# Sparse attention and a gated feed-forward layer on one core: early queries and keys in 256-byte pieces on two queues, fewer warming products, probabilities set out by any engine

## The chip, the cores and the metric

The kernel runs on one core of a Trainium2 chip. The time is device microseconds of one execution, and a kernel's time is the median of several. Five engines work side by side: TensorE (PE in the profile; its weight loads are PEld), VectorE (DVE), ScalarE (ACT), GpSimd (POOL) and SyncE (SP, which here only issues transfers). Each runs its own instructions strictly in the order of the program and waits for the others by semaphores.

## The reference

All is float32. The scores reach values at which the softmax is sharp, so the kernel keeps float32 accuracy by splitting each operand of a large product into a high part and a low rest and adding three products (high by high, high by rest, rest by high).

```
q, k, v: (8, 8, 576, 64)            # batch, head, position, width
scores = q @ k.T / 8
heads 0..3: key j counts for query i if 0 <= i - j < 32
heads 4..7: key j counts for query i if j <= i and j % 32 == i % 32
attn = softmax over the keys that count
x = (attn @ v), heads side by side  # (4608, 512)
h = x @ w_in                        # w_in (512, 2048)
g = h * clip(h + 3, 0, 6) / 6
out = g @ w_out                     # w_out (2048, 512)
```

## The kernel before

**Attention** goes by pairs of heads: `pair(g)` makes heads 2c and 2c+1 of batch b, 32 pairs in all. Pairs c = 0, 1 are local (`loc`), c = 2, 3 strided; within a batch they are taken in the order 0, 2, 1, 3 (`TURNS`). Names in the trace carry b and c: `ps_30` is the scores' bank of pair 3, its first head. For a pair, the queries and keys are loaded (`load`), stood upright (for batch 0 by TensorE against an identity, line 371, out of PSUM by the two halves of `evac`; later by DVE), multiplied (`scores`, lines 600 and 608), copied or masked into a tile `e` (lines 626, 633, 640), and made into probabilities in the steps `most`, `less`, `exp`, `total`, `inverse`, `norm` (lines 644 to 665). There are two tiles `e`, one for each head of a pair, and all pairs share them. Then the probabilities are **set out**: turned in 32 x 32 blocks and placed on the diagonal of a cleared tile (`atstr`, `atloc`), so that a few products with the values (line 735 for strided pairs, 399 and 388 for local ones, tile `pv`) give x. Batches 0 and 1 do this by DVE transposes of 32 partitions each, straight into place (`turn`, lines 684 and 687: 4 for a strided head, 6 for a local one). Batches 2 to 7 do it by one transpose in place (`flip`, line 690) and copies on ACT (`spread`, lines 697 and 700). The local pairs of batch 0 (`first`) turn by TensorE (`stand`, tile `pe`). `keep_x` splits x into its high part (ACT, line 426) and its rest (DVE, line 429), in two pieces `n` = 0, 1 for most pairs, and puts the last 64 positions by in `left`.

**Weights** come as raw bits: `weight_part` loads 512 KB (line 273), takes the number apart on ACT (lines 281, 285), joins it on DVE (line 289), casts the high part on ACT or POOL (303, 305) and makes the rest on POOL (308).

**The feed-forward layer** goes by tiles of 512 positions, one tile for each of the batches 0 to 2 (`ffn`), then by larger tiles. `first_product` makes one of 16 slices fc of h, from the four x tiles c (lines 856 to 858, three products of 128 x 512 each); line 776 and 779 are the gate, 790 and 794 the split of g (`gh`, `gl`), 833 to 835 the second product. In batch 0 the first four slices are begun before any is gated.

**The order.** Every step is given to a planner (`Plan`) as an operation with an engine (or a choice of engines), a duration that the author wrote down, the tiles that it reads and writes, and a due time. `emit` then places the operations one by one in its own clock, for each engine the earliest that can start, and the instructions of each engine stand in that order. Where its clock sees PE idle in the first 100 us, it puts in **warming products** (`idle`: once 46 small ones, line 1568, then 128 x 384 ones, line 1570). `T0` is the moment that the plan sets for the first slice of h; all later due times count from it. So a change of costs or keys early on moves instructions on every engine.

**Transfers** take one of eight completion counters in turn, whichever queue they go to. The first eight issue at once; each later one waits in its queue until the transfer eight places before it has landed, and whatever stands behind it on that engine waits too. Transfers of SP and of ACT run on the same 16 DMA engines.

Of the kernel before, what the change touches and what calls it, by code (L numbers as in the profile page):

```python
# [10 lines left out]
F32 = mybir.dt.float32  # L11
# [8 lines left out]
P = 128  # L20
# [17 lines left out]
T0 = 44.0  # L38
# [15 lines left out]
IDLE = 0.64  # L54
FETCH = 2.2
FIRST = 3.4
FEW = 46


class Plan:  # L60
# [29 lines left out]
    def emit(self, idle):  # L90
# [21 lines left out]
        while done < len(ops):  # L112
# [24 lines left out]
            if e == "PE" and t < WARM and t - free[e] > IDLE:  # L137
                for i in range(int((t - free[e]) / IDLE)):
                    order.append((free[e] + i * IDLE, len(order), None, e))
# [34 lines left out]
def attention_ffn(ctx: ExitStack, tc, q, k, v, w_in, w_out, out):  # L174
    nc = tc.nc
# [154 lines left out]
    def either(us):  # L330
        return {"POOL": us, "DVE": us}

    def zero(key, pool, shape, dtype, us, due, name):

        def go(e):
            on(e).memset(new(pool, key, shape, dtype, name), 0.0)
            if key[0] == "e":
                t = tiles[key]
                on(e).memset(t[:, :NQB * WIN].rearrange("p (u x) -> p u x", x=WIN)[:, :, 2 * PAD:], 1.0e-9)
                on(e).memset(t[:, NQB * WIN:NQB * WIN + 8 * PAD].rearrange("p (u x) -> p u x", x=PAD)[:, :, NPOS:NPOS + 1], 1.0e-9)  # L340
        op(either(us), 0, go, writes=[key], due=due)
# [63 lines left out]
    def x_keys(b, c):  # L405
        return [("x", b, c, i) for i in range(2)] if b < 2 else [raw_key(b, c)]

    def keep_x(nm, b, c, puts, due):
# [4 lines left out]
        for n, (bkey, what, place, size, rest) in enumerate(puts):  # L413
# [16 lines left out]
            kk = [lk] if rest else xk  # L430
            last = all(x[0] is not bkey for x in puts[n + 1:])
            whole = rest or b >= 2
            op("ACT", 0.15 + size * (0.0019 if strided else 0.00085), hi, reads=[bkey] + (xk if rest else []), writes=kk, give=bkey if last and whole else None, due=due + n)
            if not whole:
                op("DVE", 0.15 + size * (0.002 if strided else 0.00105), lo, reads=[bkey], writes=kk, give=bkey if last else None, due=due + 0.2 + n)
# [4 lines left out]
    def pair(g):  # L440
# [37 lines left out]
        for x in "qk":  # L478
# [6 lines left out]
            if early:  # L485
# [3 lines left out]
                def load(x=x, nkey=nkey, rows=rows, ni=ni):  # L489
                    t = new(wp, nkey, [P, 2, ni * D], F32, f"{x}n{nm}")  # L490
                    (nc.scalar if g < 2 and x == "k" else nc.sync).dma_start(
                        t[:rows], {"q": q, "k": k}[x][b, h0:h0 + 2].rearrange("j (p i) d -> p j (i d)", i=ni))
                tb = [slot(early) for _ in range(2)]

                def tr(x=x, nkey=nkey, tb=tb, rows=rows, ni=ni):
                    ps = [psum(tb[h], f"{x}p{nm}{h}") for h in range(2)]
                    half = ni // 2
                    for i in range(ni):
                        for j in range(2):
                            upright(ps[i // half], j, i % half * rows, tiles[nkey][:rows, j, D * i:D * i + D])  # L500
# [15 lines left out]
                op("ACT" if g < 2 and x == "k" else "SP", 0.55, load, writes=[nkey], due=-60 + 2 * g + (x == "k") - 900 * (g < 2 and x == "k"), after=1.15)  # L516
# [161 lines left out]
        for j in range(2):  # L678
# [9 lines left out]
            if b >= 2:  # L688
# [16 lines left out]
                op("ACT", 6 * 0.31 if loc else 4 * 0.36, spread, reads=[ekeys[j]], writes=[akeys[j]], due=due - 1.9 + j)  # L705
# [31 lines left out]
        op("PE", 1.25 * slow, values, reads=[*akeys, *vkeys], writes=[*vb, *xk, lk], take=vb, due=due - 1001,  # L737
# [80 lines left out]
    def ffn(b):  # L818
        s0, puts = start[b], []
        chunk = TILE / NFC  # L820
        xk = {c: x_keys(b, c) if b < 2 else [("x", 1, c, i) for i in range(2)] for c in range(NCC)}

# [19 lines left out]
        def first_product(fc):  # L842
# [3 lines left out]
            for n_, c in enumerate(TURNS[b]):  # L846
# [12 lines left out]
                op("PE", 0.683, mm1, reads=xk[c] + wkeys, writes=[pk],  # L859
# [744 lines left out]
```

## Time and profile before

| | us |
|---|---|
| median of 3 runs (869.94, 870.25, 876.99) | 870.25 |
| the profiled execution's own time | 871.98 |
| its span, from the first to the last instruction | 870.2 |
| PE busy | 847.4 |
| POOL, ACT, DVE busy | 616.6, 558.9, 539.0 |
| first transpose of batch 0 on PE | 8.30 |
| first product of h | 38.90 |
| end of the 48 products with which h is begun | 58.88 |

Times in the profile count from the start of the span. A float32 product appears as two passes on PE; its busy time overlaps with the next one's, so PE's speed is read from the distance of starts and not from the durations. A wait in brackets is the idle time of the engine just before the instruction and what ended it; `issue` means that the profile shows nothing that was waited for.

### The profile page before, as it was taken

The page shows a single profiled execution, that of the slowest core. Times are in us where ns is not written, and L with a number is a line of the kernel's source. Part 1 is how long each engine was busy: PE and PEld are TensorE (multiplying, and loading weights), DVE is VectorE, ACT ScalarE, POOL GpSimd, SP SyncE. Part 2 cuts the span into 40 slices and gives each one's busy share as a digit, 9 for nine tenths or more (in the row PEclk, how much of TensorE's full clock was granted, in tenths as well). Part 3 has the DMA queues.
Part 4 walks back from the last instruction along what each step waited for, and adds up shares of the span by engine and source line. Part 5 has one row for each costly group of instructions (what it writes and reads, how often), then busy time and mean ns, then how long its engine had stood idle before and what let it go on. Part 6 is the DMA issues. An engine that isn't in the chain of part 4 may idle for free.

```text
span 870.2 us, 18946 instructions
## 1 busy us (share of the span) xinstructions
PE 847.4 (97%) x6962; PEld 683.8 (79%) x6962; DVE 539.0 (62%) x898; ACT 558.9 (64%) x1246; POOL 616.6 (71%) x606
## 2 busy tenths in 40 slices
PE   8889999999999999999999999999999999999996
PEld 6667777887888788888888878788888778888884
DVE  5688878344454538454546664466767888555586
ACT  3687657678778865877677965776744645454441
POOL 4688877587547799766676994465975987767673
PEclk9999999999999999999999999999999999999998
DMA  8968723898984455898999897877666667866636
GB/s 194 330 138 233 234 41 73 210 281 245 279 234 108 128 129 141 233 266 233 269 277 289 274 301 214 237 204 189 183 202 193 185 180 222 240 202 192 183 122 145
DMA packets 323308, 179.12 MB, mean 206 GB/s; under 512 B 182864, under 2 KB 300368, under 8 KB 323216
## 3 DMA queue, kind: packets, MB, share of 16 engines
q1 hardware_dynamic: 318564, 176.27, 71.5%
q10 hardware_dynamic: 4652, 1.64, 0.9%
q8 instruction: 55, 0.90, 0.4%
q14 instruction: 37, 0.30, 0.1%
HBM read 136.97 MB, written 40.89 MB: 204 GB/s over the span
## 4 chain that ended last, share of the span: by engine, by line
PE 82%; DMA 5%; POOL 5%; DVE 4%; ACT 2%; issue 1%; SPq 0%; POOLq 0%; DVEq 0%; ACTq 0%
PE P L1129 8%; PE P L1130 8%; PE P L1131 8%; PE cP L1452 5%; PE cP L1453 5%; PE cP L1454 5%; PE acc L833 5%; PE ph L856 5%; PE ph L857 4%; PE ph L858 4%; PE acc L835 4%; PE acc L834 4%; PE acc L1214 3%; PE acc L1215 3%; PE acc L1216 3%; PE pv L399 2%
## 5 line engine op out<-in xcount | busy, mean ns | idle before, releaser
L1470 DVE SCALAR_TENSOR_TENSOR C<-cP,C 128x512 f32<-128x512 f32 x96 | 65.7, 687 | 40.4 <-PE cP L1454 39.5
L794 POOL TENSOR_TENSOR gl<-u,gh 128x512 fp32r<-128x512 f32 x48 | 65.2, 1361 | 33.3 <-ACT gh L790 17.1
L1141 DVE TENSOR_TENSOR G<-P,G 128x512 f32<-128x512 f32 x64 | 44.0, 689 | 65.6 <-PE P L1131 53.2
L1129 PE MATMUL P<-B_T,wr 128*128 128x512 f32 x192 | 76.1, 396 | 3.9 <-ACT G L1136 2.3
L833 PE MATMUL acc<-wo,gh 128*128 128x512 f32 x192 | 77.2, 402 | 0.0
L835 PE MATMUL acc<-wo,gl 128*128 128x512 f32 x192 | 75.2, 392 | 0.3 <-POOL gl L794 0.2
L834 PE MATMUL acc<-wo,gh 128*128 128x512 f32 x192 | 74.9, 390 | 0.0
L1130 PE MATMUL P<-B_T,wr 128*128 128x512 f32 x192 | 74.8, 390 | 0.0
L1131 PE MATMUL P<-B_T,wr 128*128 128x512 f32 x192 | 74.8, 390 | 0.0
L1136 ACT COPY G<-P 128x512 f32<-128x512 f32 x64 | 37.6, 587 | 52.2 <-PE P L1131 51.7
L1367 POOL TENSOR_TENSOR sp<-G,sp 128x512 fp32r<-128x512 f32 x34 | 47.6, 1411 | 24.6 <-ACT sp L1363 22.5
L665 POOL TENSOR_TENSOR e<-e,st 128x144 f32<-128x144 f32 (+1 forms) x64 | 44.9, 704 | 20.7 <-DVE st L661 15.2
L779 DVE SCALAR_TENSOR_TENSOR u<-u,ph 128x512 f32<-128x512 f32 x48 | 32.8, 684 | 38.0 <-ACT u L776 37.8
L856 PE MATMUL ph<-x,wi 128*128 128x512 f32 x128 | 52.5, 410 | 2.3 <-ACT x L426 1.2
L857 PE MATMUL ph<-x,wi 128*128 128x512 f32 x128 | 50.8, 397 | 1.4 <-DVE x L429 0.8
L700 ACT COPY atloc<-e 32x192 f32<-32x192 f32 x144 | 50.8, 353 | 1.9 <-DVE e L690 0.3
L776 ACT ACTIVATE u<-ph,three 128x512 f32<-128x512 f32 x48 | 33.0, 687 | 28.1 <-PE ph L858 27.8
L858 PE MATMUL ph<-x,wi 128*128 128x512 f32 x128 | 50.8, 397 | 0.0
L644 DVE TENSOR_REDUCE st<-e 128x8 f32<-128x144 f32 (+1 forms) x64 | 25.6, 412 | 35.8 <-POOL e L640 35.6
L1129 PE MATMUL P<-B_B,wr 128*128 128x512 f32 x120 | 47.1, 392 | 0.0
L1130 PE MATMUL P<-B_B,wr 128*128 128x512 f32 x120 | 46.8, 390 | 0.0
L1129 PEld LDWEIGHTS P<-B_T,wr 128*128 128x128 f32 x192 | 36.0, 188 | 13.7 <-ACT G L1136 3.6
(604 smaller groups left out, 2672.6 us busy)
## 6 DMA issues: line engine op xcount, KB each, us to landing
wr<-dA SPq DMA_DIRECT2D x72, 256.0 KB
or<-do SPq DMA_DIRECT2D x32, 512.0 KB
wr<-dSu SPq DMA_DIRECT2D x48, 256.0 KB
wr<-dSv SPq DMA_DIRECT2D x48, 256.0 KB
or<-do SPq DMA_DIRECT2D x48, 256.0 KB
rawi<-in_moe_w_in_dram SPq DMA_DIRECT2D x16, 512.0 KB
rawo<-in_moe_w_out_dram SPq DMA_DIRECT2D x16, 512.0 KB
do<-wo SPq DMA_DIRECT2D x16, 512.0 KB
```

What stands on the lines that cost most here:

```text
L700: nc.scalar.copy(at[PAD * (a + h):PAD * (a + h) + PAD, :, rows], e[rows, :, PAD * h:PAD * h + PAD])
L794: (nc.vector if tail else nc.gpsimd).tensor_tensor(out=to, in0=src(), in1=tiles[gk[0]].bitcast(F32), op=ALU.subtract)
L833: nc.tensor.matmul(acc, gh, woh, start=fc == 0, stop=False)
L834: nc.tensor.matmul(acc, gh, wol, start=False, stop=False)
L835: nc.tensor.matmul(acc, gl, woh, start=False, stop=end)
L856: nc.tensor.matmul(ph, wih, xh, start=n_ == 0, stop=False)
L857: nc.tensor.matmul(ph, wih, xl, start=False, stop=False)
L858: nc.tensor.matmul(ph, wil, xh, start=False, stop=n_ == NCC - 1)
L1129: nc.tensor.matmul(ph, wh, xh, start=fresh and k == 0, stop=False, skip_group_check=not fresh)
L1130: nc.tensor.matmul(ph, wh, xl, start=False, stop=False, skip_group_check=not fresh)
L1131: nc.tensor.matmul(ph, wl, xh, start=False, stop=k == 1, skip_group_check=not fresh)
L1470: nc.vector.scalar_tensor_tensor(out=tiles[ck], in0=tiles[bank], scalar=1.0 / 6.0, in1=tiles[ck], op0=ALU.mult, op1=ALU.add)
```

## The change

1. The queries and keys of batch 0 are loaded into a tile of [partition, i, head, 64] instead of [partition, head, i x 64], by two transfers of one head each instead of one of both. A contiguous run in the tile is 256 bytes, where it was 1536 (local) or 2048 (strided). The keys of the first three pairs go by ACT's queue, where it was those of the first two.
2. Warming products are counted from 2.6 us on and not from the start of PE's idle time.
3. Strided pairs of batch 0 and all pairs of batch 1 set the probabilities out by `flip` and single copies (4 or 6 a head), each an operation of its own that ACT, POOL or DVE may take, and POOL resets a column of a strided `e` (`again`).
4. The two pieces of an x tile of batches 0 and 1 have keys of their own, so in the plan the second high part does not wait for the first rest, and the copies into `left` are due 3 us later.
5. `T0` is 43 instead of 44.

```diff
-T0 = 44.0
+T0 = 43.0
+FREE = 2
+LEFTS = 3.0
+BEGIN = 2.6
...
-                for i in range(int((t - free[e]) / IDLE)):
+                for i in range(int((t - max(free[e], BEGIN)) / IDLE)):
...
-            kk = [lk] if rest else xk
+            kk = [lk] if rest else xk if whole else [("xh", b, c, n)] + ([] if n else xk)
...
-                op("DVE", 0.15 + size * (0.002 if strided else 0.00105), lo, reads=[bkey], writes=kk, give=bkey if last else None, due=due + 0.2 + n)
+                op("DVE", 0.15 + size * (0.002 if strided else 0.00105), lo, reads=[bkey, ("xh", b, c, n)], writes=[("xl", b, c, n)], give=bkey if last else None, due=due + 0.2 + n)
...
-                    t = new(wp, nkey, [P, 2, ni * D], F32, f"{x}n{nm}")
-                    (nc.scalar if g < 2 and x == "k" else nc.sync).dma_start(
-                        t[:rows], {"q": q, "k": k}[x][b, h0:h0 + 2].rearrange("j (p i) d -> p j (i d)", i=ni))
+                    t = new(wp, nkey, [P, ni, 2, D], F32, f"{x}n{nm}")
+                    for j in range(2):
+                        (nc.scalar if g < 3 and x == "k" else nc.sync).dma_start(
+                            t[:rows, :, j], {"q": q, "k": k}[x][b, h0 + j].rearrange("(p i) d -> p i d", i=ni))
...
-            if b >= 2:
+            if b >= 2 or b == 1 or b == 0 and not loc:
...
-                op("ACT", 6 * 0.31 if loc else 4 * 0.36, spread, reads=[ekeys[j]], writes=[akeys[j]], due=due - 1.9 + j)
+                if b < FREE:
+                    for a in range(n // PAD):
+                        for h in range(1 + loc):
+                            def set_out(e, a=a, h=h, j=j):
...
+                                if e == "ACT":
+                                    nc.scalar.copy(at, x)
+                                else:
+                                    on(e).tensor_copy(at, x)
...
+                            op({"ACT": 0.33, "POOL": 0.42, "DVE": 0.37} if loc else {"ACT": 0.4, "POOL": 0.5, "DVE": 0.44}, 0, set_out,
+                               reads=[ekeys[j], ("zero",) + akeys[j]], writes=own, due=due - 1.9 + j)
+                else:
+                    op("ACT", 6 * 0.31 if loc else 4 * 0.36, spread, reads=[ekeys[j]], writes=[akeys[j]], due=due - 1.9 + j)
```

Where this moves instructions is seen in the order of each engine. **The start of ACT.** Tiles `kn` are the keys of batch 0, by pair. Before:

```order
L491 DMA kn_0_136<-in_k_dram 96x2x384
L491 DMA kn_2_188<-in_k_dram 72x2x512
L513 ACT_TABLE_LOAD
L513 COPY qplain<-qp_01_275 128x3x96 [waits PE_49]
L513 COPY kplain<-kp_01_298 128x3x96 [waits PE_49]
```

Now, with DMAHW0 and DMAHW2 the counters of the two halves of `kn_0`:

```order
L495 DMA kn_0_137<-in_k_dram 96x6x64 x2
L495 DMA kn_2_234<-in_k_dram 72x8x64 x2
L495 DMA kn_1_246<-in_k_dram 96x6x64 [waits DMAHW0_49]
L495 DMA kn_1_246<-in_k_dram 96x6x64 [waits DMAHW2_49]
L517 ACT_TABLE_LOAD
L517 COPY qplain<-qp_01_273 128x3x96 [waits PE_49]
L517 COPY kplain<-kp_01_292 128x3x96 [waits PE_49]
```

The keys of pair 1 moved here from SP, wait for those of pair 0, and stand ahead of the table load and the first copies. On PE the 7 wide warming products ahead of the first transpose become 3 (15 wide ones in all become 5), and the scores of pair 0 stand ahead of the transposes of `kn_2`.

**DVE around the second strided head of pair 2** (`st_2`, its tile `e_228`, now `e_226`) and the masks of pair 1's scores (`ps_10`, `ps_11`). Before:

```order
L661 RECIPROCAL st_2_508<-st_2_508 128x8
L684 STREAM_TRANSPOSE atstr_269<-e_130 32x8x32 x4
L658 TENSOR_REDUCE st_2_508<-e_228 128x8
L633 TENSOR_TENSOR e_130<-ps_10_599,mband 96x6x64
L635 MEMSET e_130 32x32
L661 RECIPROCAL st_2_508<-st_2_508 128x8
L644 TENSOR_REDUCE st_1_677<-e_130 96x6
L633 TENSOR_TENSOR e_228<-ps_11_600,mband 96x6x64
```

Now:

```order
L665 RECIPROCAL st_2_505<-st_2_505 128x8
L662 TENSOR_REDUCE st_2_505<-e_226 128x8
L665 RECIPROCAL st_2_505<-st_2_505 128x8
L694 STREAM_TRANSPOSE e_130<-e_130 128x256
L720 COPY atstr_262<-e_130 32x8x32
L694 STREAM_TRANSPOSE e_226<-e_226 128x256
L637 TENSOR_TENSOR e_130<-ps_10_585,mband 96x6x64
L639 MEMSET e_130 32x32
L637 TENSOR_TENSOR e_226<-ps_11_586,mband 96x6x64
```

The second head's reciprocal moved ahead of the mask that waits for PE, and the four transposes became one with one copy.

**POOL around pair 3**, the last of batch 0 (`st_3`), and the rests of the first weights (`wi` by c, `wo` by fc). Before:

```order
L305 CAST wi_838<-fi_689 128x512
L648 TENSOR_TENSOR e_130<-e_130,st_3_785 128x8x18
L648 TENSOR_TENSOR e_228<-e_228,st_3_785 128x8x18
L308 TENSOR_TENSOR wi_838<-fi_689,wi_838 128x512
L308 TENSOR_TENSOR wi_840<-fi_727,wi_840 128x512
L1537 MEMSET vloc 32x128
L665 TENSOR_TENSOR e_130<-e_130,st_3_785 128x8x18
L665 TENSOR_TENSOR e_228<-e_228,st_3_785 128x8x18
L308 TENSOR_TENSOR wi_917<-fi_828,wi_917 128x512
```

Now:

```order
L669 TENSOR_TENSOR e_130<-e_130,st_3_776 128x8x18
L669 TENSOR_TENSOR e_226<-e_226,st_3_776 128x8x18
L720 COPY atstr_262<-e_130 32x8x32 x2
L1558 MEMSET vloc 32x128
L720 COPY atstr_262<-e_130 32x8x32
L308 CAST wi_909<-fi_744 128x512
L707 MEMSET e_130 128x8
L720 COPY atstr_267<-e_226 32x8x32 x2
L311 TENSOR_TENSOR wi_909<-fi_744,wi_909 128x512
L707 MEMSET e_226 128x8
L311 TENSOR_TENSOR wi_944<-fi_893,wi_944 128x512
```

The rests of c = 1 (`wi_838`, now `wi_909`) and c = 2 moved behind the last normalisation, and POOL took five of the eight copies. On PE the products of pair 3 with its values now stand ahead of all products of h for c = 2, 1 and 3 (36 products); before, 33 of the 48 stood ahead of them. The order of PE's last 1133 instructions, DVE's last 232, ACT's last 219, POOL's last 128 and SP's last 181 is the same in both.

More of the change, by code (lines that the diff above doesn't have):

```diff
@@ L340, in go @@
                 on(e).memset(t[:, NQB * WIN:NQB * WIN + 8 * PAD].rearrange("p (u x) -> p u x", x=PAD)[:, :, NPOS:NPOS + 1], 1.0e-9)
-        op(either(us), 0, go, writes=[key], due=due)
+        op(either(us), 0, go, writes=[key, ("zero",) + key], due=due)
     def timing(g):
@@ L429, in lo @@
                 nc.vector.tensor_tensor(out=to(1), in0=what(tiles[bkey.key]), in1=to(0).bitcast(F32), op=ALU.subtract)
-            kk = [lk] if rest else xk
             last = all(x[0] is not bkey for x in puts[n + 1:])
             whole = rest or b >= 2
-            op("ACT", 0.15 + size * (0.0019 if strided else 0.00085), hi, reads=[bkey] + (xk if rest else []), writes=kk, give=bkey if last and whole else None, due=due + n)
+            kk = [lk] if rest else xk if whole else [("xh", b, c, n)] + ([] if n else xk)
+            op("ACT", 0.15 + size * (0.0019 if strided else 0.00085), hi, reads=[bkey] + (xk if n or rest else []), writes=kk, give=bkey if last and whole else None, due=due + n + LEFTS * rest)
             if not whole:
-                op("DVE", 0.15 + size * (0.002 if strided else 0.00105), lo, reads=[bkey], writes=kk, give=bkey if last else None, due=due + 0.2 + n)
+                op("DVE", 0.15 + size * (0.002 if strided else 0.00105), lo, reads=[bkey, ("xh", b, c, n)], writes=[("xl", b, c, n)], give=bkey if last else None, due=due + 0.2 + n)
     def pair(g):
@@ L499, in tr @@
                         for j in range(2):
-                            upright(ps[i // half], j, i % half * rows, tiles[nkey][:rows, j, D * i:D * i + D])
+                            upright(ps[i // half], j, i % half * rows, tiles[nkey][:rows, i, j])
                 def evac(e, x=x, tb=tb, h=0):
@@ L515, in evac @@
                         nc.vector.tensor_copy(to, ps)
-                op("ACT" if g < 2 and x == "k" else "SP", 0.55, load, writes=[nkey], due=-60 + 2 * g + (x == "k") - 900 * (g < 2 and x == "k"), after=1.15)
+                op("ACT" if g < 3 and x == "k" else "SP", 1.3, load, writes=[nkey], due=-60 + 2 * g + (x == "k") - 900 * (g < 3 and x == "k"), after=1.3)
                 op("PE", 0.13 * ni * slow, tr, reads=[("ident",), nkey, "plain"], writes=tb, take=tb, due=due - 1020, mode="s")
@@ L736, in values @@
                                      ats[j][:, i].rearrange("p (a m) -> p a m", a=4)[:, :, :NPOS], start=True, stop=True)
-        op("PE", 1.25 * slow, values, reads=[*akeys, *vkeys], writes=[*vb, *xk, lk], take=vb, due=due - 1001,
+        op("PE", 1.25 * slow, values, reads=[*akeys, *vkeys] + [(x, i) for x in akeys for i in range(8) if b < FREE], writes=[*vb, *xk, lk], take=vb, due=due - 1001,
            room=0.0 if early else ROOM, mode="v")
@@ L821, in ffn @@
         xk = {c: x_keys(b, c) if b < 2 else [("x", 1, c, i) for i in range(2)] for c in range(NCC)}
+        parts = {c: [(x, b, c, n) for x in ("xh", "xl") for n in range(3)] if b < 2 else [] for c in range(NCC)}
         def mm2(fc, gk):
@@ L858, in mm1 @@
                     nc.tensor.matmul(ph, wil, xh, start=False, stop=n_ == NCC - 1)
-                op("PE", 0.683, mm1, reads=xk[c] + wkeys, writes=[pk],
+                op("PE", 0.683, mm1, reads=xk[c] + parts[c] + wkeys, writes=[pk],
                    due=s0 + (fc + n_ * 0.12) * chunk, mode="f")
```

5 lines of the change are left out of this document (added).

## The prediction

> **What bounds the kernel now.** I read the page's head, then busy times by stage, then PE's instructions in order of time, then the waits of the engines behind the stage that loses time.
>
> ```profile
> span 870.2 us, 18946 instructions
> ...
> PE 847.4 (97%) x6962; PEld 683.8 (79%) x6962; DVE 539.0 (62%) x898; ACT 558.9 (64%) x1246; POOL 616.6 (71%) x606
> ...
> core 0: us, PE busy (x) PEld busy (x) DVE busy (x) ACT busy (x) POOL busy (x), PEclk, DMA share, GB/s
> 8.30:38.90 30.60, 25.72 (x654) 20.83 (x653) 19.32 (x48) 17.52 (x44) 11.73 (x15) 0.94 0.93 259
> 38.90:50.45 11.55, 10.66 (x118) 7.76 (x118) 9.36 (x20) 9.89 (x23) 9.79 (x14) 1.00 0.95 301
> 50.45:58.88 8.43, 6.74 (x48) 5.00 (x48) 5.94 (x9) 6.62 (x13) 7.54 (x6) 0.81 0.54 111
> 58.88:97.55 38.67, 38.12 (x378) 29.79 (x377) 33.71 (x64) 28.81 (x53) 34.60 (x31) 1.00 0.75 216
> 97.55:144.26 46.71, 45.89 (x505) 36.55 (x505) 35.32 (x70) 28.72 (x52) 37.30 (x35) 1.00 0.40 88
> 144.26:560.00 415.74, 414.64 (x3656) 335.50 (x3655) 215.54 (x386) 304.17 (x767) 296.68 (x324) 1.00 0.80 226
> 560.00:870.20 310.20, 298.64 (x1507) 243.93 (x1505) 214.51 (x293) 161.90 (x298) 212.87 (x161) 0.99 0.66 190
> ```
>
> From 58.88 to 560 PE stands idle for 2.5 us in all (0.55, 0.82 and 1.10 in the three rows): it is the bound there, and its work does not change. After 560 it idles 11.6 us, but the order there is mostly the same in both kernels. So the change is worth what it does to the moment at which PE's dense work begins, less what PE waits later because another engine did not move up as far. That moment is the end of the 48 products with which h is begun:
>
> ```profile
> 2.79 5.58 PE L1570 MATMUL idle<-ident 128*128 128x384 f32 x14
> 8.30 1.21 PE L371 MATMUL qp<-ident,qn 96*64 96x96 f32 x24
> ...
> 12.43 0.97 PE L608 MATMUL ps<-kplain,qplain 64*32 64x64 f32 x72
> ...
> 15.32 1.21 PE L371 MATMUL kp<-ident,kn 96*64 96x96 f32 x24
> ...
> 26.89 1.52 PE L608 MATMUL ps<-kt,qt 64*32 64x64 f32 x72
> ...
> 33.41 1.01 PE L600 MATMUL ps<-kt,qt 64*64 64x36 f32 x53
> ...
> 50.45 1.22 PE L735 MATMUL pv<-atstr,v 128*64 128x72 f32 x32
> ...
> 58.88 0.48 PE L856 MATMUL ph<-x,wi 128*128 128x512 f32 x1
> ...
> 61.05 0.40 PE L833 MATMUL acc<-wo,gh 128*128 128x512 f32 x1
> ...
> 64.23 0.39 PE L835 MATMUL acc<-wo,gl 128*128 128x512 f32 x1
> ```
>
> The warming products (14 passes) fill PE until the first transpose at 8.30. The products of pair 3 with its values come at 50.45, the 48 are done at 58.88. A large product costs (64.23 - 61.05) / 14 = 0.227 us at full clock.
>
> **The change part by part.** First the loads and the warming.
>
> ```profile
> 5.72 0.33 SPq L377 DMA_DIRECT2D v<-in_v_dram  x1
> ...
> DMA packets 916, 1.36 MB, mean 272 GB/s; under 512 B 136, under 2 KB 631, under 8 KB 916
> ...
> q1 hardware_dynamic: 1906, 0.61, 97.0%
> ...
> q1 hardware_dynamic: 1435, 0.42, 90.3%
> ...
> 1.89 1.28 ACT L513 ACT_TABLE_LOAD   x1 [1.89 <-issue]
> ```
>
> SP's first load of values waits for the first transfer of keys, so those had landed by 5.72, 2.6 us before PE turned to them: the warming held PE, not the data. Three wide products end at 2.79 + 6 x 5.51 / 14 = 5.15. Then the data decide. The large runs moved at 272 GB/s (from 3 to 8 us); 590 KB of pair 0 take 2.2 us at that, so start and landing take 5.72 - 2.2 = 3.5. A load now is 2 x 96 x 6 = 1152 pieces. The trace has 256-byte pieces in the loads of values: from 26 to 28 us an engine spent 16 x 2 x 0.903 / 1435 = 20.1 ns on a packet, from 13 to 17 us 16 x 4 x 0.970 / 1906 = 32.6 ns. I take 23, near the first, whose queue was full as this one will be; both ends stay for the range. Then 2304 pieces take 3.3 us, and the four pairs' loads land at 6.8, 10.1, 13.4 and 16.8 in the order in which PE wants them (ends: first 6.4 or 8.2, third 12.2 or 17.6). PE: transposes of pair 0 at 6.8 (1.03 us each, the distance of such groups), the queries of pair 2 at 10.1, scores at 11.1 instead of 12.43, keys of pair 1 at 14.4 instead of 15.32. **0.9 us earlier**, which goes on into the softmax of pair 0, because its exponential stands behind the copy of these keys on ACT.
>
> The Trainium skill, "DMA: Bandwidth & Descriptors", section Specifications, asks for at least 512 bytes a transfer and says that smaller ones are read, modified and written. The two packet rows agree (a piece of 256 bytes at 20 to 33 ns in 16 engines is 126 to 204 GB/s, against 272); followed to its end the rule gives the late landing below.
>
> ACT's wait is new: the keys of pair 1 wait there for those of pair 0 (6.8), and the table load (1.28) and the first copies stand behind. With two issues (0.33, as in SP's row) ACT is free at 8.8; two copies after the keys' transposes end near 10.3, before the scores' 11.1. It costs nothing while pair 2's queries land later than 9.3, else what is left of it. On SP the values and weights wait longer, as each waits for a transfer of the larger load; the added 4.5 us of DMA time (8 x 1152 pieces at 23 ns / 16 = 13.2 us, for 2.36 MB at 272 GB/s = 8.7 us) are covered as long as the weights for the second product are used only after 53 us; the DMA share falls to 0.54 in 50.45 to 58.88, so the load that ends near 48 would end near 52.5. Without that cover each us is one of PE.
>
> Then the order of the softmax.
>
> ```profile
> 3.69 0.11 POOL L230 MEMSET mtri<- 128x18 f32 x1
> ...
> 29.11 0.17 DVE L661 RECIPROCAL st<-st 128x8 f32<-128x8 f32 x1
> ...
> 30.31 1.75 DVE L684 STREAM_TRANSPOSE atstr<-e 32x256 f32<-32x256 f32 x4
> ...
> 32.93 0.54 DVE L644 TENSOR_REDUCE st<-e 96x6 f32<-96x384 f32 x1
> ...
> 33.61 0.82 POOL L648 TENSOR_TENSOR e<-e,st 96x384 f32<-96x384 f32 x1 [2.88 <-PE pv L735]
> ...
> 39.42 0.82 POOL L665 TENSOR_TENSOR e<-e,st 96x384 f32<-96x384 f32 x1
> ...
> 41.95 2.54 POOL L308 TENSOR_TENSOR wi<-fi,wi 128x512 fp32r<-128x512 f32 x2
> ...
> 44.58 1.57 POOL L665 TENSOR_TENSOR e<-e,st 128x144 f32<-128x144 f32 x2
> ...
> 48.27 1.78 DVE L684 STREAM_TRANSPOSE atstr<-e 32x256 f32<-32x256 f32 x4
> ```
> ```profile
> L690 DVE STREAM_TRANSPOSE e<-e 128x256 f32<-128x256 f32 x24 | 10.4, 439 | 9.2 <-POOL e L665 9.2
> L697 ACT COPY atstr<-e 32x256 f32<-32x256 f32 x96 | 38.6, 402 | 8.7 <-DVE e L690 7.8
> L305 POOL CAST wi<-fi 128x512 fp32r<-128x512 f32 x8 | 6.8, 852 | 3.2 <-DVE fi L289 3.2
> L289 DVE SCALAR_TENSOR_TENSOR fi<-fi,rawi 128x512 int32<-128x512 int32 x16 | 17.3, 1086 | 1.7 <-ACT rawi L285 1.6
> L303 ACT CAST wi<-fi 128x512 fp32r<-128x512 f32 x8 | 4.9, 618 | 3.7 <-DVE fi L289 3.6
> L308 POOL TENSOR_TENSOR wi<-fi,wi 128x512 fp32r<-128x512 f32 x16 | 22.2, 1394 | 1.7 <-ACT wi L303 1.3
> ```
>
> Pair 1's scores come at 26.0 (26.89 less 0.9). The reciprocal of pair 2's second head was stuck at 29.11 behind the mask that waits for them; now it goes ahead, at 26.2. Its setting out took until 32.06 on DVE; now a flip of 0.44 and eight copies on three engines end at 29.2. A copy on POOL does not occur: between ACT's 0.40 and the POOL cast's 0.85, I take 0.45, since it has half the cast's columns. With DVE free, pair 1's second head is reduced at 29.7 and not at 32.93, POOL's subtraction goes from 33.61 to 30.4, its normalisation from 39.42 to 34.4 (in front of it stand one cast and one rest of a weight, 2.2 us). Pair 3's scores now precede pair 2's values on PE, 28.9 instead of 33.41. Its two normalisations waited behind two rests (41.95 to 44.49); now they come at 37.6 and 38.3. Setting out: flip, a weight join (1.09), copy, flip, then copies, five of eight on POOL with a cast between them; done at 42.5 instead of 50.05. **Pair 3's values at 42.6 instead of 50.45.**
>
> That is not the gain, since 36 of the 48 products now stand behind them where 15 did. They need weights whose parts were put off: join of c = 2 on DVE after the last flip, copy and rest of x, 41.9 to 42.9; cast on ACT behind another step there, 43.7; rest on POOL, 43.9 to 45.3. PE's third product starts there; 33 more at 0.227 end at 53.0. Those of c = 1 and 3 and the rest of x (46.9) are ready before PE comes to them (47.6 for c = 3), so the two pieces of x side by side add nothing of their own. Between 38.9 and 45.3 PE has little but the two value products, 2.4 us. Before, a stretch with 1.7 us of idle time (50.45 to 58.88) ran at a mean clock of 0.81, which is 1.6 us lost; I add 1.6 here. **54.6 instead of 58.88: 4.3 us.**
>
> Last, POOL. Up to g's eighth rest (97.55) it has 11 copies, 6 resets (0.11, as the small MEMSET) and 2 casts more, 3 weight rests less: 4.95 + 0.66 + 1.7 - 4.18 = +3.1 us, against 4.07 of idle time in 58.88 to 97.55. Up to the sixteenth (144.26) another 8.5 (6 copies, 2 resets, 4 rests, a normalisation, less a cast), against 9.41. DVE, from which the transposes go, has more room. POOL can keep up, but hardly ahead of before by the whole 4.3. Give-back: nothing to 4.3; I take 1.0, as the slack covers the work in both rows.
>
> The sum: 4.3 - 1.0 = **3.3 us**. The profiled execution took 871.98 us, 1.78 outside the span, and stands 1.73 above the median of 870.25. It would take 868.7, and the median 867.0.
>
> **Rivals.**
>
> *Late landing (slower).* Pieces cost more than I take. Everything to 58.88 hangs on the keys of pair 1, third in line: each us by which they land after 13.4 comes off the gain. At 16.7 nothing is left, that is from (16.7 - 3.5) x 16 / 6912 = 30.6 ns a piece. The 13-to-17 row has 32.6: landing 17.6, 0.9 slower, 871.2; with values and weights late behind them up to 873. For it: the DMA share of 0.93 and 0.95 to 50.45, so nothing is hidden. Against: in that row the pieces were issued in waits. Chance 0.18.
>
> *PE starts cold.* With 5 wide warming products and 1.7 us idle before 6.8, the transposes may run at half clock: two groups of 1.03 cost 2.1 more, of which 1.2 hides in the wait for pair 2's queries, so 0.9 is lost and the median is 867.9; if the scores run slow too (0.97), 868.9. The Trainium skill, "TensorE: Matmul & The Clock Gate", Part 1, gives the clock a window of about 3.4 us of activity; that fits the 1.6 us lost above, and by it the shorter warming would be paid for. Chance 0.15.
>
> *POOL takes all.* Copies at 0.85 add 4.4 by the eighth rest, more than its slack; PE then waits for rests until about 144 and the gain is 0: 870.2. Chance 0.12. That the small pieces themselves do nothing, since the warming alone held the start, changes no time here but which part earns it.
>
> *More.* No cold stretch and no give-back: 1.6 + 1.0 more, 864.4, and to 862.5 if waits for instructions in the start go too. Chance 0.13.
>
> **How the numbers follow.** The forecast, 865 to 868.5, has 0.42. The rivals from 862.5 to 871.5 make it up to more than 8 in 10; left out are the late landing's far end and gains over 7.7. This kernel's runs tell about 1%, 8.7 us, from no change: that is above any case, so faster 0.03, same 0.95, slower 0.02.
>
> **What the profile will show.** First transpose near 6.8 and keys of pair 1 transposed near 14.4 (later than 16.5: late landing); clock below 1.00 before 12 us (cold); pair 3's values near 42.6; the 48 products done near 54.6; PE idle for POOL's rests of g between 58 and 145 (under 1 us: no give-back). If values of pair 3 come early and the 48 products do not, the put-off weights were mis-sized. A waiting time of PE after 150 us that was not there would make all of it wrong.

## The result and the profile after

| | before | changed |
|---|---|---|
| median, us | 871.36 (869.94 to 876.99, 6 runs) | 880.46 (878.55 to 882.17, 6 runs) |
| ratio, 95% interval | 1 | 1.0102 (1.0080 to 1.0123) |
| span of the profiled execution | 870.2 | 879.5 |
| PE busy | 847.4 | 847.7 |
| end of the 48 products | 58.88 | 55.75 |

The change made the kernel 9 us slower; 867.0 was predicted, with a range to 871.5. PE's busy time is nearly the same, but made up otherwise: fewer warming products and more time at half clock. So the loss is read by stages, from idle time and clock. The windows of the changed kernel (columns as in the prediction) are cut at the same events at first: first transposes, first product of h, products of pair 3 with its values, end of the 48:

```profile
6.60:33.27 26.67, 21.77 (x629) 18.72 (x628) 15.52 (x41) 17.39 (x43) 13.65 (x23) 0.88 0.75 199
33.27:42.51 9.24, 6.20 (x113) 4.76 (x111) 6.67 (x17) 7.61 (x21) 5.99 (x13) 0.99 0.96 353
42.51:55.75 13.24, 12.52 (x67) 9.71 (x68) 4.92 (x7) 8.86 (x18) 10.53 (x10) 0.74 0.92 274
55.75:100.00 44.25, 40.67 (x387) 31.29 (x386) 37.90 (x53) 33.60 (x66) 40.68 (x41) 1.00 0.74 206
100.00:150.00 50.00, 45.31 (x490) 35.23 (x489) 34.33 (x65) 32.15 (x65) 36.42 (x39) 0.93 0.39 87
150.00:569.30 419.30, 416.71 (x3658) 335.55 (x3657) 216.34 (x384) 305.99 (x770) 297.35 (x325) 1.00 0.80 222
569.30:879.50 310.20, 299.32 (x1512) 244.99 (x1510) 216.40 (x292) 159.32 (x291) 212.09 (x161) 0.99 0.67 192
```

The start came 3.13 us earlier. From 55.75 to 150 PE idles 3.58 + 4.69 = 8.27 us, where before had 0.55 + 0.82 from 58.88 to 144.26; and a clock of 0.93 over 50 us is another 3.5 lost. Of the rest, 150 to 569 idles 2.59 (1.10 before), the end 10.88 (11.56). The sum is -3.13 + 6.90 + 3.50 + 1.49 - 0.68 = 8.1 of the 9.3.

The waits of PE from 58 to 150 us (in total, times, longest), the changed kernel first and that of before behind it, show who was late:

```profile
PE ph L877 <- POOL wi L308: 3.0, 1, 3.0
PE ph L879 <- POOL wi L311: 2.0, 4, 0.8
PE acc L856 <- POOL gl L814: 1.8, 1, 1.8
PE ph L877 <- DVE u L799: 0.8, 1, 0.8
PE ps L612 <- DVE kplain L537: 0.4, 1, 0.4
```
```profile
PE ph L856 <- DVE u L779: 1.1, 2, 0.8
PE acc L835 <- POOL gl L794: 0.2, 1, 0.2
```

Weights are late: their casts (308) and rests (311). The longest wait, on PE's own rows:

```profile
126.54 0.39 PE L879 MATMUL ph<-x,wi 128*128 128x512 f32 x1
129.97 0.79 PE L877 MATMUL ph<-x,wi 128*128 128x512 f32 x1 [3.04 <-POOL wi L308]
...
132.24 0.63 PE L877 MATMUL ph<-x,wi 128*128 128x512 f32 x1
132.67 0.63 PE L878 MATMUL ph<-x,wi 128*128 128x512 f32 x1
```

After it the starts stand 0.43 us apart and not 0.23, until 135.66: half clock (0.50 granted from 130 to 134 us). It costs another 3.4 us, so this wait is paid a second time.

### The profile page after: what moved, and what is told of

Same layout as the page of the kernel before. It is cut to its first block, busy times and chain, and to the rows that moved or that the text cites. A ratio compares the mean times of both kernels' runs of the same rounds, so it can differ in the third digit from the quotient of the medians.

```text
span 879.5 us, 18954 instructions
## 1 busy us (share of the span) xinstructions
PE 847.7 (96%) x6942; PEld 683.5 (78%) x6942; DVE 536.9 (61%) x870; ACT 564.9 (64%) x1268; POOL 622.0 (71%) x632
## 4 chain that ended last, share of the span: by engine, by line
PE 82%; POOL 6%; DVE 4%; DMA 3%; issue 2%; ACT 2%; SPq 1%; POOLq 0%; DVEq 0%; ACTq 0%
PE P L1150 8%; PE P L1151 8%; PE P L1152 8%; PE cP L1473 5%; PE cP L1475 5%; PE cP L1474 5%; PE ph L877 5%; PE ph L879 4%; PE acc L854 4%; PE ph L878 4%; PE acc L856 4%; PE acc L855 4%; PE acc L1235 3%; PE acc L1237 3%; PE acc L1236 3%
## 5 line engine op out<-in xcount | busy, mean ns | idle before, releaser
L877 PE MATMUL ph<-x,wi 128*128 128x512 f32 x128 | 54.2, 424 | 3.9 <-POOL wi L308 3.0
L879 PE MATMUL ph<-x,wi 128*128 128x512 f32 x128 | 52.6, 411 | 2.7 <-POOL wi L311 2.7
L669 POOL TENSOR_TENSOR e<-e,st 96x384 f32<-96x384 f32 (+1 forms) x64 | 41.8, 658 | 17.3 <-DVE st L665 13.3
L878 PE MATMUL ph<-x,wi 128*128 128x512 f32 x128 | 52.0, 406 | 0.0
L1150 PE MATMUL P<-B_B,wr 128*128 128x512 f32 x120 | 47.5, 396 | 1.7 <-DVE u_6c L799 1.6
L1151 PE MATMUL P<-B_B,wr 128*128 128x512 f32 x120 | 46.9, 391 | 0.0
L1152 PE MATMUL P<-B_B,wr 128*128 128x512 f32 x120 | 46.8, 390 | 0.0
```

The source lines that it names most:

```text
L877: nc.tensor.matmul(ph, wih, xh, start=n_ == 0, stop=False)
L878: nc.tensor.matmul(ph, wih, xl, start=False, stop=False)
L879: nc.tensor.matmul(ph, wil, xh, start=False, stop=n_ == NCC - 1)
L1150: nc.tensor.matmul(ph, wh, xh, start=fresh and k == 0, stop=False, skip_group_check=not fresh)
L1151: nc.tensor.matmul(ph, wh, xl, start=False, stop=False, skip_group_check=not fresh)
L1152: nc.tensor.matmul(ph, wl, xh, start=False, stop=k == 1, skip_group_check=not fresh)
```

## The experiments

Differences are taken between ratios to the kernel before, which was measured beside each group (0.1% is 0.87 us). By the intervals in the table a difference of two of them is uncertain by 0.2 to 0.4%, some 3 us. "Idle" is PE's idle time from 58 to 150 us and "cold" what half clock cost there, both summed from 46 windows of 2 us of one profile.

| run | median | ratio (95%) | idle | cold |
|---|---|---|---|---|
| before | 871 | 1 | 1.4 | 0.5 |
| changed | 880.46 | 1.0102 (1.0080 to 1.0123) | 8.3 | 3.4 |
| e1_start | 880.17 | 1.0104 (1.0075 to 1.0132) | 8.0 | 5.1 |
| e2_batch0 | 877.49 | 1.0075 (1.0048 to 1.0102) | 9.4 | 3.4 |
| f2_old_order | 869.89 | 0.9985 (0.9969 to 1.0001) | 1.5 | 0 |
| i1_warm | 870.95 | 0.9995 (0.9978 to 1.0012) | 1.6 | 0 |
| n1_T445 | 870.07 | 0.9996 (0.9981 to 1.0012) | 1.9 | 0 |
| n2_T43 | 874.19 | 1.0038 (1.0011 to 1.0064) | 1.3 | 1.4 |
| n3_after_T435 | 886.71 | 1.0176 (1.0145 to 1.0207) | 7.8 | 5.1 |
| n4_join100 | 876.96 | 1.0065 (1.0046 to 1.0085) | 3.5 | 3.4 |
| h1_after_costs | 874.80 | 1.0056 (1.0031 to 1.0081) | 5.2 | 0 |
| x_nopool | 874.22 | 1.0039 (1.0022 to 1.0055) | 2.3 | 0 |
| e3_dve_reduce | 876.89 | 1.0064 (1.0036 to 1.0092) | 7.3 | 3.4 |
| e4_pool_small | 878.43 | 1.0084 (1.0059 to 1.0110) | 6.8 | 5.1 |
| g1_after_joins | 868.40 | 0.9971 (0.9951 to 0.9990) | 3.4 | 3.4 |
| g0_before_joins | 866.71 | 0.9953 (0.9938 to 0.9969) | 1.0 | 0 |
| g2_e1_joins | 871.03 | 1.0005 (0.9989 to 1.0021) | 2.6 | not readable |
| p1_rows | 878.48 | 1.0071 (1.0045 to 1.0096) | 7.2 | 3.4 |
| p2_rows_reduce | 877.73 | 1.0074 (1.0051 to 1.0096) | 7.8 | 3.4 |
| f3_T445 | 867.41 | 0.9975 (0.9953 to 0.9996) | 1.3 | 0.2 |

The profile of g2_e1_joins shows one clock, 0.95, from end to end, so the cold time is not read from it.

**Which part loses the time?** e1_start is the kernel before with the loads, ACT's queue and the shorter warming:

```diff
+                    for j in range(2):
+                        (nc.scalar if g < 3 and x == "k" else nc.sync).dma_start(
+                            t[:rows, :, j], {"q": q, "k": k}[x][b, h0 + j].rearrange("(p i) d -> p i d", i=ni))
...
-                op("ACT" if g < 2 and x == "k" else "SP", 0.55, load, writes=[nkey], due=-60 + 2 * g + (x == "k") - 900 * (g < 2 and x == "k"), after=1.15)
+                op("ACT" if g < 3 and x == "k" else "SP", 1.3, load, writes=[nkey], due=-60 + 2 * g + (x == "k") - 900 * (g < 3 and x == "k"), after=1.3)
...
+                for i in range(int((t - max(free[e], BEGIN)) / IDLE)):
```

> The kernel before with parts 1 and 2 of the change alone (loads in 256-byte pieces, ACT's queue for the keys of three pairs, shorter warming), T0 44, probabilities set out as before. If the time was lost to the copies (on DVE, by a shared port with POOL, or on POOL, by their load), none are here: the start gains up to 0.9 us and nothing is given back, 869 to 871. If it was lost to the rows that a new plan puts in front of the weights in the queues, any new order can lose or gain, and 865 to 876 are all possible; then PE's waits between 58 and 145 us differ from the 1.3 us of before.

It lost all of the 9 us, with not one copy in it. So the copies, on which two of the three theories rested (a port shared with POOL, POOL's load), were not needed for the loss.

e2_batch0 is the changed kernel without the copies of batch 1:

```diff
-FREE = 2
+FREE = 1
...
-            if b >= 2 or b == 1 or b == 0 and not loc:
+            if b >= 2 or b == 0 and not loc:
```

> The changed kernel, but batch 1 is set out by transposes as before; copies only for the strided pairs of batch 0. Copies (port or load): those that run between 58 and 145 us are gone, PE's waits there fall from 8 us to about 1.3, and what the start gained stays: 866 to 869. Order: another order, with its own waits; 866 to 880, the waits at other places.

Not 866 to 869, but 877.5: without the copies of batch 1, a wait of 4.34 us for a cast stands at 128.76.

f2_old_order is e1_start with the old numbers in the plan; the instructions are the new ones:

```diff
-                op("ACT" if g < 3 and x == "k" else "SP", 1.3, load, writes=[nkey], due=-60 + 2 * g + (x == "k") - 900 * (g < 3 and x == "k"), after=1.3)
+                op("ACT" if g < 2 and x == "k" else "SP", 0.55, load, writes=[nkey], due=-60 + 2 * g + (x == "k") - 900 * (g < 2 and x == "k"), after=1.15)
```

> Parts 1 and 2 (256-byte pieces, keys of three pairs on ACT's queue, shorter warming) with the order of before on every engine: in the plan the loads keep their old durations and engines. Loads themselves cost: the small pieces or what they push back on SP cost the time, 876 or more as in e1_start. Order: the rows stand as before, nothing of the 10 us is lost, 869.5 to 872, earlier by what of the 0.9 us of the start goes through this order.

This settles it. The same loads and the same warming in the old order lose nothing; between f2_old_order and e1_start stand only the numbers (and the engine noted for one load) by which the planner orders the rows, and 1.2%. The instructions of DVE and POOL stand in f2_old_order exactly as in before. i1_warm takes the warming alone:

```diff
-                for i in range(int((t - free[e]) / IDLE)):
+                for i in range(int((t - max(free[e], BEGIN)) / IDLE)):
```

> The kernel before with the shorter warming alone, same order, old loads. If the warming held the start, PE begins its transposes near 6 us, and what f2_old_order won (0.5 to 1.5 us) is won here too: 869 to 870. If the data hold it (keys of pair 1, third in line), nothing: 870 to 872.

Nothing that can be measured; the loads' own share (0.9985 against 0.9995) is not either.

**Is any other order as bad?** n1_T445 and n2_T43 change `T0` of the kernel before, n3_after_T435 that of the changed one:

```diff
-T0 = 44.0
+T0 = 44.5
```
```diff
-T0 = 44.0
+T0 = 43.0
```
```diff
-T0 = 43.0
+T0 = 43.5
```

> The kernel before with T0 at 44.5 and nothing else: the same operations, other places in the queues. Order: the 870 of before is a fortunate order and another one takes 873 to 881, with 3 us or more of new waits of PE in 58 to 145 us. Start or copies: nothing of the change is in it, 870 to 872.

> The kernel before with part 5 of the change alone, T0 at 43. Order: 873 to 881, waits at other places than with 44.5. Start or copies: 870 to 872.

> The changed kernel with T0 at 43.5: the same operations in another order. Order: the time moves by some us in either direction, 872 to 884, and PE's waits in 58 to 145 us stand at other places. Copies (port or load): all copies are still there, 879 to 882.

The first two told less than I had expected of them: in the plan that they make, nearly all rows that move stand after 145 us (ahead of that, one rest of x on DVE near 117 us in n1_T445 and one clearing on POOL in n2_T43), and idle time before that stays at that of before. n2_T43 lost 0.4% all the same, and its cause is open. n3_after_T435 moved by 6 us for half a microsecond in one number. Its rows are those of the changed kernel up to 115 us, yet its first second product comes at 51.69 and not at 55.75. So the start differs by 4 us between executions of the same rows, and an early one is no mark of this order.

n4_join100 moves rows in the stretch itself, in the kernel before:

```diff
-        op("DVE", 1.05, join, reads=[key], writes=[fkey], due=due - 3)
+        op("DVE", 1.00, join, reads=[key], writes=[fkey], due=due - 3)
```

> The kernel before with one number of the plan changed: a join is noted as 1.00 us and not as 1.05. Nothing of the change is in it, but the rows between 45 and 145 us stand otherwise (n1_T445 and n2_T43 moved rows only after 145 us). Order: 873 or more, PE's idle time in 58 to 150 us 4 us or more where before has 1.4. Copies, port of the copies, load, small pieces: 870 to 872.

It lost 0.65%, at places of its own. The next two keep the copies and give another order: h1_after_costs is the changed kernel with the one line of f2_old_order, x_nopool offers the copies to ACT and DVE alone:

```diff
-                            op({"ACT": 0.33, "POOL": 0.42, "DVE": 0.37} if loc else {"ACT": 0.4, "POOL": 0.5, "DVE": 0.44}, 0, set_out,
+                            op({"ACT": 0.33, "DVE": 0.37} if loc else {"ACT": 0.4, "DVE": 0.44}, 0, set_out,
```

> The changed kernel, but the plan keeps the old durations of the early loads (0.55 and 1.15 in place of 1.3 and 1.3) and the old engine of pair 1's keys; they are issued as in the change. Order: another order, in whose clock the ninth slice comes at 93.2 (changed 94.6, before 91.4), 872 to 880. Copies (port or load): all copies are there, 878 to 882.

> The changed kernel with the copies offered to ACT and DVE alone; the plan is made anew. Load of POOL: nothing is added to POOL but the resets, PE's idle time in 58 to 150 us under 3 us, 866 to 870. Order: in the plan's own clock the ninth slice of h comes at 91.7, as before (91.4), where the changed kernel has 94.6, so here too 866 to 871; it tells order from load only if the time stays at 876 or more, which would speak against both.

Both are better than the changed kernel and worse than before. x_nopool missed its 866 to 871: it repairs the stretch to 150 us, but idles 1.8 us from 150 to 400, where before had none. An order is a draw, and that of before is among the good ones.

**By what does an order lose it?** e3_dve_reduce and e4_pool_small keep each row of the changed kernel in its place:

```diff
-                                    on(e).tensor_copy(at, x)
+                                    if e == "DVE":
+                                        nc.vector.tensor_reduce(out=at, in_=x.unsqueeze(3), axis=AX.X, op=ALU.max)
+                                    else:
+                                        nc.gpsimd.tensor_copy(at, x)
```

> The changed kernel with the same order of rows on every engine; each copy that DVE took is done by a reduction over an axis of one element, which moves the same numbers. Port: the copy of 3.24 us at 93.77 and the others that were stretched come down to 0.4, POOL's rests come 2 to 3 us sooner, PE's waits at 95 and 130 us shrink, 4 us or more faster than the changed kernel (876 or less). Load and order: DVE's copies get shorter, PE waits as before, within 1 us of 880.5.

```diff
-                                    on(e).tensor_copy(at, x)
+                                    if e == "POOL" and b == 1:
+                                        nc.gpsimd.tensor_copy(at[:, :, :1], x[:, :, :1])
+                                    else:
+                                        on(e).tensor_copy(at, x)
```

> The changed kernel with the same order of rows; the copies of batch 1 that POOL took write one column in place of 32 (the rest of those blocks stays cleared, so that part of the output is left out). Load: some 8 copies of 0.38 to 0.53 us become 0.1, POOL is up to 3 us ahead by 145 us, PE's waits for POOL shrink by 2 us or more: 878 or less. Port and order: within 1 us of 880.5.

e4_pool_small leaves part of the output out. DVE's copies cost 0.38%, 3.3 us, POOL's 0.18%, 1.6 us: both less than expected by their theory, the second not clear of noise, and together not what was lost. But they point at DVE beside POOL. In e1_start PE's first long wait is for a gate on DVE:

```profile
91.13 0.80 PE L858 MATMUL ph<-x,wi 128*128 128x512 f32 x1 [3.98 <-DVE u L781]
```

Where it comes from, in DVE's rows and POOL's:

```profile
81.00 4.19 DVE L290 SCALAR_TENSOR_TENSOR fi<-fi,rawi 128x512 int32<-128x512 int32 x1
85.12 0.64 DVE L430 TENSOR_TENSOR x<-pv,x 128x256 fp32r<-128x256 f32 x1
85.66 2.50 DVE L290 SCALAR_TENSOR_TENSOR fi<-fi,rawi 128x512 int32<-128x512 int32 x1
88.09 2.27 DVE L689 STREAM_TRANSPOSE atloc<-e 32x192 f32<-32x192 f32 x6
90.39 0.69 DVE L781 SCALAR_TENSOR_TENSOR u<-u,ph 128x512 f32<-128x512 f32 x1
```
```profile
80.52 1.31 POOL L309 TENSOR_TENSOR wo<-fo,wo 128x512 fp32r<-128x512 f32 x1
81.78 1.29 POOL L796 TENSOR_TENSOR gl<-u,gh 128x512 fp32r<-128x512 f32 x1
83.03 0.83 POOL L667 TENSOR_TENSOR e<-e,st 96x384 f32<-96x384 f32 x1
83.81 0.83 POOL L650 TENSOR_TENSOR e<-e,st 96x384 f32<-96x384 f32 x1
84.59 1.79 POOL L309 TENSOR_TENSOR wo<-fo,wo 128x512 fp32r<-128x512 f32 x1
86.34 1.27 POOL L309 TENSOR_TENSOR wi<-fi,wi 128x512 fp32r<-128x512 f32 x1
```

A join, 0.65 us elsewhere, took 4.19 while POOL went from one instruction to the next, and the next took 2.50. The rest on POOL at 84.59, in which the first join ended, took 1.79 and not 1.3. The transposes and the gate behind are not slowed, but they are late. The Trainium skill, "SBUF — State Buffer", section "Who interferes with whom", says that DVE and GpSimd share a pair of ports to SBUF, that an instruction of DVE with two inputs in SBUF contends with one of GpSimd that reads SBUF, as a copy in a faster mode does, and that a reduction never contends. The rows agree: the joins have two inputs in SBUF, while the rest of x at 85.12, which reads `pv` from PSUM, took 0.64 beside a busy POOL. That POOL holds the join is read from these rows; what follows shows what it is worth. g1_after_joins (868.4, its idle and cold time not all gone) takes the joins away from the order of the changed kernel, with the copies by reduction too; g0_before_joins and g2_e1_joins do it in the orders of before and of e1_start, and all three leave the low bits of the weights out:

```diff
-            nc.vector.scalar_tensor_tensor(out=f, in0=f, scalar=3, in1=bits(),
-                                           op0=ALU.logical_shift_left, op1=ALU.bitwise_or)
+            nc.vector.tensor_reduce(out=f, in_=f.unsqueeze(2), axis=AX.X, op=ALU.max)
```

> The changed kernel, same order, with no two-input instruction and no plain copy left on DVE between 58 and 145 us: the copies as in e3_dve_reduce, and each join of a weight's bits by a reduction over one element of the same size (the low bits are left out, so the numbers are not the reference's). Port: the joins that took up to 2.6 us take 0.65, and PE's idle time in 58 to 150 us (8.3 in the changed kernel, 7.3 in e3_dve_reduce) falls under 3 us, 872 or less. Order: the rows still stand behind the same waits, idle time 5 us or more, 874 to 878.

> The kernel before, same order, with each join of a weight's bits by a reduction over one element (the low bits are left out). Port: in this order PE waits only 1.4 us between 58 and 150 us though joins are stretched there too, so there is little to win: 867 to 871. Order by other waits: shorter joins help every order alike, 12 us as in the changed one: 857 to 862.

> The order of e1_start (880.2; no copies in it) with the same joins by reduction. Port: the join of 4.19 us and its followers go, PE's idle time in 58 to 150 us falls from 8 us to under 3: 868 to 872. Order by other waits: 876 or more.

The joins of the whole execution (count, busy, mean ns) before, in the changed kernel, in e1_start and in g2_e1_joins; for before, the first of the two rows stands in the prediction (17.3 us):

```profile
L289 DVE SCALAR_TENSOR_TENSOR fo<-fo,rawo 128x512 int32<-128x512 int32 x16 | 14.7, 930 | 0.7 <-ACT rawo L285 0.6
```
```profile
L292 DVE SCALAR_TENSOR_TENSOR fi<-fi,rawi 128x512 int32<-128x512 int32 x16 | 18.4, 1164 | 1.4 <-ACT rawi L288 1.4
L292 DVE SCALAR_TENSOR_TENSOR fo<-fo,rawo 128x512 int32<-128x512 int32 x16 | 13.7, 862 | 4.7 <-ACT rawo L288 3.2 <-issue 1.5
```
```profile
L290 DVE SCALAR_TENSOR_TENSOR fi<-fi,rawi 128x512 int32<-128x512 int32 x16 | 20.7, 1299 | 2.5 <-ACT rawi L286 1.6 <-POOL wo L309 1.0
L290 DVE SCALAR_TENSOR_TENSOR fo<-fo,rawo 128x512 int32<-128x512 int32 x16 | 14.8, 944 | 0.1
```
```profile
L290 DVE TENSOR_REDUCE fi<-fi 128x512 int32<-128x512 int32 x16 | 10.6, 670 | 0.4 <-ACT fi L282 0.4
L290 DVE TENSOR_REDUCE fo<-fo 128x512 int32<-128x512 int32 x16 | 10.4, 670 | 0.1
```

Joins are held in every order: 32.0 us before, 32.1 in the changed kernel, 35.5 in e1_start, and 21.0 where none is held. So the changed kernel does not hold them longer than before did; what an order decides is whether PE is short of what stands behind a held one. The ratios give the size roughly: without the joins before gains 0.47%, 4.1 us, the changed order 0.93% (e3_dve_reduce to g1_after_joins), 8.1 us, and that of e1_start 0.99%, 8.6 us.

The place is shown better by the stretch from the first second product to the 192nd, in one profile each, as it leaves the start out:

| run | first second product, us | from there to the 192nd, us |
|---|---|---|
| before, f2_old_order, f3_T445 | 60.36, 56.14, 59.34 | 93.0, 93.0, 92.8 |
| g0_before_joins | 58.31 | 91.6 |
| e1_start | 58.07 | 103.0 |
| g2_e1_joins | 56.81 | 92.6 |
| changed, e4_pool_small, p1_rows | 55.75, 54.84, 51.58 | 105.0, 104.7, 104.3 |
| e3_dve_reduce | 54.03 | 104.2 |
| g1_after_joins | 50.33 | 99.1 |

PE's work in it is the same but for products of h: 153 in the order of before, 150 in that of e1_start, 159 in the changed one. At 0.227 us each, e1_start loses 10.7 us in this stretch and the changed kernel 10.6. Without the joins e1_start gets 10.4 of it back: there, held joins are the loss. Before gets 1.5. The changed kernel gets 0.8 back with DVE's copies and 5.2 more with the joins; 4.7 stay, and the wait at 118.64 below with the half clock behind it (2.45 and 3.4 us) is as large. That the profile of g1_after_joins is shorter than that of before all the same is owed to its start. The median of g2_e1_joins stays 4.5 us above that of g0_before_joins, and its profile, of a faster execution, does not show where.

One thing is not separated: the reduction does not read the low bits, so DVE does not wait for ACT's second step either. From 58 to 150 us that wait is 1.6 us in e1_start, and 3.2 in the changed kernel against 1.1 in g1_after_joins.

**The second place.** Near 130 us PE waits even in g1_after_joins (2.45 us at 118.64). There DVE has masks, which wait for scores, ahead of two joins, and POOL two subtractions ahead of the cast. p1_rows puts the two joins with their casts, rests and steps on ACT ahead of them; p2_rows_reduce does it with e3_dve_reduce. In `emit`, 747 is the first mask, the others are the two weights' steps:

```diff
-        for _, _, n, e in sorted(order):
+        rows = [(n, e) for _, _, n, e in sorted(order)]
+        first = [(n, self.by[n]) for n in (334, 335, 340, 341, 336, 342, 337, 338, 343, 344)]
+        rows = [r for r in rows if r not in first]
+        at = [n for n, _ in rows].index(747)
+        rows[at:at] = first
+        for n, e in rows:
```

> The changed kernel with rows moved at one place: two joins on DVE ahead of the masks that wait for scores near 125 us, with their casts and rests on POOL ahead of the two subtractions, and their two steps on ACT ahead of the exponentials. Nothing else moves, PE's order is the same. Order at this place: the wait of 3.04 us at 129.97 falls under 1 us and the half clock after it (3.4 us) goes, 5 to 6.5 us less: 874 to 876. If the place is only where time that is missing elsewhere shows up: PE waits the same a few products later, 879 to 881.

> p1_rows with e3_dve_reduce (876.9): if the two are separate causes they add up, 870 to 872, as before; if the same time is counted twice, 875 to 877.

The wait of 3.04 us for the cast is gone; what is left at this place is 0.42 for the rest behind it (0.47 in the changed kernel). Another wait came a few products later:

```profile
123.74 0.50 PE L884 MATMUL ph<-x,wi 128*128 128x512 f32 x1 [0.42 <-POOL wi L316]
...
131.83 0.50 PE L882 MATMUL ph<-x,wi 128*128 128x512 f32 x1 [4.17 <-DVE u L804]
```

The gate of the slices that PE had finished at 127.5 stood behind the softmax on ACT:

```profile
126.52 0.53 ACT L661 ACTIVATE e<-e 96x384 f32<-96x384 f32 x1 [0.26 <-POOL e L657]
128.69 1.08 ACT L723 COPY atloc<-e 32x192 f32<-32x192 f32 x3 [1.64 <-DVE e L699]
129.79 0.66 ACT L289 ACTIVATE fo<-rawo 128x512 f32<-128x512 f32 x1
130.36 1.25 ACT L801 ACTIVATE u<-ph,three 128x512 f32<-128x512 f32 x2
```

p1_rows came to 1.0071, 2.7 us of the 5 to 6.5 expected and within the uncertainty of none, with runs from 873.3 to 879.3; p2_rows_reduce gained nothing over e3_dve_reduce. Its profile is of one of the faster runs: the span is 6.3 us shorter than the changed kernel's, but 4.2 of these are won by the first second product, up to which both have the same rows; from there to the 192nd only 0.7:

```profile
40.26 1.72 PE L760 MATMUL pv<-atstr,v 128*64 128x72 f32 x30 [2.00 <-POOL atstr L725]
...
51.58 0.39 PE L859 MATMUL acc<-wo,gh 128*128 128x512 f32 x1
```

So the wait only moved. I take the place to be not two rows but the softmax of a whole pair, which stands ahead of the gate; an order without it was not tried, so this is not shown.

**A better version.** f3_T445 is f2_old_order with a later `T0`:

```diff
-T0 = 44.0
+T0 = 44.5
```

> f2_old_order with T0 at 44.5, which moves rows only after 145 us. Start gain of f2 kept in another late order: 867 to 870, under 0.9975 of before if both the start gain and the late order count, 0.998 to 1.000 otherwise.

0.9975 (0.9953 to 0.9996): 1.3% faster than the changed kernel and 0.25% faster than before, which its interval just tells from nothing; with as many orders tried as here, that can be chance.

## Why the prediction was wrong

- *Loads and warming: right, in part by luck.* The first transposes came at 6.60 (6.8 forecast), scores of pair 0 at 11.17 (11.1), keys of pair 1 at 14.11 (14.4). But only two transposes found their data at 6.60; the others waited for the queries until 8.04, and pair 2's queries, transposed from 9.91 on (10.1 forecast), did not hold them up again. No late landing as large as the rival's; the clock stayed at 1.00 up to 20 us, so no cold start. The rows of PE:

```profile
6.60 0.38 PE L374 MATMUL qp<-ident,qn 96*64 96x96 f32 x2
8.04 1.12 PE L374 MATMUL qp<-ident,qn 96*64 96x96 f32 x21 [1.06 <-DMA qn<-in_q_dram]
...
11.17 0.97 PE L612 MATMUL ps<-kplain,qplain 64*32 64x64 f32 x72
...
14.11 1.16 PE L374 MATMUL kp<-ident,kn 96*64 96x96 f32 x24
```

- *The softmax: right, and closer than one execution can tell.* Pair 3's values at 42.51 (42.6), the third product at 45.56 (45.3); in p1_rows, with the same rows up to there, the values came at 40.26:

```profile
42.51 1.21 PE L755 MATMUL pv<-atstr,v 128*64 128x72 f32 x30 [2.01 <-POOL atstr L720]
...
45.56 0.79 PE L879 MATMUL ph<-x,wi 128*128 128x512 f32 x1 [0.72 <-POOL wi L311]
...
55.75 0.39 PE L854 MATMUL acc<-wo,gh 128*128 128x512 f32 x1
```

- *The 48 products: 55.75 and not 54.6.* The clock of 0.74 from 42.51 cost 3.4 us, where 1.6 was taken from before. The gain was 3.1, not 4.3. In other executions of the same rows it was more: the first second product, at 55.75 here, came at 54.84 in e4_pool_small, 51.69 in n3_after_T435 and 51.58 in p1_rows. So the start was forecast well, and the loss behind it is larger than 9 us by as much as the start won.
- *The step that failed: "Give-back: nothing to 4.3; I take 1.0, as the slack covers the work in both rows".* It was over 12 us (3.1 gained, 9 lost), by waits of PE behind held joins, DVE's copies and a softmax that stood ahead of the weights' rows, and by half clock. Three things are wrong in it. I set POOL's work against its idle time, as if an idle microsecond could be used wherever it stands; up to 127.16 us POOL idles 2.85 us ahead of two subtractions that wait for DVE, and the cast for which PE waits stands behind them. I bounded the loss by the gain: no order of the rows could cost more than the start had brought, and no rival of mine let the middle be later than before. And a wait of PE was counted once, though half clock can follow: 3.4 us behind the wait of 3.04.
- *The copies.* POOL's cost what I took (0.51 for strided and 0.36 for local blocks in 58 to 150 us, 0.45 forecast). So it was not *POOL takes all*, which needed 0.85. DVE's have no price in the prediction, which only said that DVE has more room. From 50 to 150 us they took 0.78 and 0.83 in the mean, and one 3.24:

```profile
93.77 3.24 DVE L720 COPY atloc<-e 32x192 f32<-32x192 f32 x1
```
```profile
L720 DVE COPY atloc<-e 32x192 f32<-32x192 f32 x8 | 6.7, 833 | 0.2
L720 DVE COPY atstr<-e 32x256 f32<-32x256 f32 x5 | 3.9, 777 | 0.1
```

- *What would make it wrong* was named in part: over 1 us of waits for POOL's rests of g between 58 and 145 (1.8 us; the other 5.0 us of waits for POOL are for casts and rests of weights, which were not named), and a new wait after 150 (1.60 us at 480.61, for a gate).

## What to carry to other kernels

Where a planner writes the order of every engine, as here, an edit has two effects, its own and that of the new order, and the second can be the larger: hold the old order (here by leaving the old numbers in the plan) to measure the first, and change one number without meaning to measure the second. A stretch in which several engines are nearly full has no slack to be added up; ask for each waiting row what is queued behind it. In this kernel VectorE's joins of two operands in SBUF and its plain copies lost time beside long runs of GpSimd; the copies done as reductions, which read one operand and move the same numbers, took at most 0.42 us.

## What was not expected of the hardware

- An instruction on DVE can be held up over several of POOL's: 4.19 us for one of 0.65. Thirteen copies of DVE took 10.6 us between 50 and 150 us, and the same as reductions 4.9, none over 0.42. The transposes which they replaced had stayed at 0.37 and 0.44.
- Half clock can follow a wait of under 2 us, or not. In p1_rows the wait of 1.83 us at 91.57 was followed by a clock of 0.50 and 0.65 in the next two windows of 2 us; in the changed kernel the same wait, 1.84 us at 95.71, by full clock.
- Executions of the same rows differ by 4 us before the dense work begins: the first second product came at 55.75 and 54.84 where the clock from 40 to 50 us was 0.69 and 0.66 (changed, e4_pool_small), and at 51.69 and 51.58 where it was 0.83 (n3_after_T435, p1_rows).
